# A short convolution and a maxout FFN on one core: the order of set-up work and first loads is changed

## The chip, the cores and the metric

The kernel runs on one core of a Trainium2 chip. The metric is the device time of one execution in microseconds. The engines of the core are named as the profile names them: PE (TensorE, matmuls; PEld is its weight load), DVE (VectorE), ACT (ScalarE), POOL (GpSimd) and SP (SyncE, which here does nothing but issue DMAs). Each engine works through its own instructions in order and waits on semaphores for the others.

## The reference

The input is x with 8 batches of 4160 rows of 192 channels. Eight heads of 24 channels each have 7 weights; a softmax over the 7 gives a causal filter that runs along the rows. The result goes through a maxout FFN with three input matrices.

```
w = exp(weight - max(weight)); w = w / (sum(w) + 1e-09)       # (8 heads, 7 taps)
y[b, s, h*24:(h+1)*24] = sum over k of w[h, k] * x_pad[b, s + k, h*24:(h+1)*24]
y = y.reshape(33280, 192)
h = maximum(maximum(y @ w1, y @ w2), y @ w3)                   # 192 -> 768
out = h @ w_out                                                # 768 -> 192
```

## The kernel before

The 33280 rows are cut into 65 blocks of 512 rows. For each block the kernel loads x, casts it to f16, runs the convolution as matmuls with a banded matrix of the softmax weights, and then two layers of matmuls. The maxout is rewritten: with wd = w1 - w3 and w2 - w3, h = y w3 + max(relu(y(w1 - w3)), y(w2 - w3)), and the part y w3 w_out is folded into a small matrix m = w3 w_out that is made once on the chip. So layer 1 (`l1`) needs two products per slice of 128 hidden channels, `top` takes relu on ACT and max on DVE, and layer 2 (`st2`) adds the hidden part and the m part in PSUM.

The first four blocks (`NDENSE = 4`) go another way, because they come before the pipeline is filled. Their x lies in five overlapping chunks of up to 112 rows (`chunks_of`). `cast_dense` (L211) writes the f16 copy into two tiles `xz[t][0]` and `xz[t][1]`, which must be zero where no channel of a head lies; blocks 2 and 3 use the tiles of blocks 0 and 1 again. `conv_dense` (L378) runs 80 matmuls of the chunks against `band`, and ACT and DVE evacuate the result into `yd` (L383). `l1_dense` (L526) then makes the layer-1 products of blocks 0 and 1.

From block 4 on, x lies in 16 pieces of 32 rows with overlap, in two halves of the partitions, in float32 buffers `xf`. There are seven such buffers (`XBUF = 7`). In the buffers of blocks 4 and up, partitions 32 to 63 must be zeroed before the load, since only some of them are written by it. `zero_x` does that, either as a copy of zeros on ACT (L137) or as a memset on a given engine (L134). The load of a block from 4 on is two DMAs of 234 KB (one for each half of the partitions). `cast_x` (L194, POOL) casts a buffer to f16.

The order of work on every engine is written out by hand (`manual_schedule`): what is issued first in the program runs first on its engine. All loads and stores go through the one queue of SP, in the order of the program, except the 7 softmax weights of each head (`wk`), which ACT issues. A load that has to wait for a zeroed buffer therefore holds up all DMAs that come after it in the program.

The set-up, in the order of the program:

- The loads: `wk` on ACT; then on SP x0 (420 KB in two DMAs), `load_wa` (L223: rows 0 to 127 of w3, w1 and w2, here columns 0 to 255), `load_wb` (L227: the other 64 rows), x1 (420 KB), the remaining columns of the weights, w_out (`wos`), x2 and x3.
- POOL makes an identity matrix. DVE zeroes `idle` (L247), `line` (L259), the two tiles `xz[0]` (L261) and `band` (L263).
- `keep_warm` issues matmuls on zeros so that PE is not idle: five of them before the softmax and three after the band matmuls.
- The softmax: maximum on DVE (L268), exp on ACT (L269, which makes the activation table be loaded first), sum (L271), reciprocal (L272) and the scaled filter `line` (L274) on DVE.
- 38 small matmuls (L283) spread `line` into the band pattern; ACT copies 28 of their columns and DVE 10 into the four row groups of `band` (L287).
- Between these, ACT zeroes buffers 4 and 5, and DVE zeroes the two tiles `xz[1]` (L276) and casts x0 (L211).

After the set-up come the dense products. `make_wd` (L302) subtracts w3 from w1 and w2 on DVE or POOL, `copy_w3` (L306), `cast_w3` (L310) and `cross_wd` (L313) move weights to where a product needs them, `transpose_w3` and `make_m` make m, and `first_hidden` is layer 2 of block 0. In the kernel before, buffer 6 is zeroed around the first `conv_dense`, and the loads of buffers 4, 5 and 6 are issued right after it. Then come the main loop over the blocks from 2 on, in which `conv` (L357), `l1` (L503) and `st2` (L567) are interleaved; `turn` (L411) transposes the convolution's result by DMA and `double` (L420, POOL) copies it to the other half of the partitions. The convolution of blocks 5 and 6, the first that needs their buffers, runs in the step of block 3.

Of the kernel before, what the change touches and what calls it, by code (L numbers as in the profile page):

```python
# [10 lines left out]
FP32 = mybir.dt.float32  # L11
FP16 = mybir.dt.float16
AXX = mybir.AxisListType.X
AF = mybir.ActivationFunctionType

P = 128
KW = 7
PAD = KW - 1
NHEAD = 8
GRP = 24  # L20
BAND_W = 128 + PAD
# [7 lines left out]
def kernel(  # L29
# [12 lines left out]
    nc = tc.nc  # L42
# [43 lines left out]
    NDENSE = 4  # L86
# [3 lines left out]
    NR = NBLK // TOK // 2  # L90
# [3 lines left out]
    def rows_of(t):  # L94
        rows = [(b, S + o) for (b, S, N, off) in blocks[t] for o in range(0, N, TOK)]
        assert len(rows) == 2 * NR
        return rows

    const = ctx.enter_context(tc.tile_pool(name="const", bufs=1))
# [10 lines left out]
    psp = ctx.enter_context(tc.tile_pool(name="psp", bufs=2, space=bass.MemoryType.PSUM))  # L110
# [5 lines left out]
    xin, xbuf, XBUF, loaded = {}, [], 7, set()  # L116

    def get_x(t):

        if not 0 <= t < NB or t in xin:  # L120
            return
        if t < XBUF:
            xbuf.append(const.tile([P, NR, D], FP32, name=f"xf_{t}"))
        xf = xbuf[t % XBUF if t < NDENSE + XBUF else NDENSE + (t - NDENSE - XBUF) % 3]
        assert all(v[0] is not xf for v in xin.values())
        xin[t] = [xf, 0, ()]

    def zero_x(t, q0=0, q1=NR, eng=None):

        if t >= NDENSE:  # L130
            get_x(t)
        xf = xbuf[t]
        if eng is not None:
            eng.memset(xf[TOK:HALF, q0:q1, :], 0.0)  # L134
            return
        zero = idle[TOK:HALF, 0:D]
        nc.scalar.copy(out=xf[TOK:HALF, q0:q1, :],  # L137
                       in_=bass.AP(tensor=zero.tensor, offset=zero.offset,
                                   ap=[list(zero.ap[0]), [0, q1 - q0], [1, D]]))

    def load_x(t, eng=nc.sync):
        if not 0 <= t < NB:
            return
        loaded.add(t)
        get_x(t)
        xf = xin[t][0]
        if t < NDENSE:
            todo = [(0, c[3], c[1] * SEQ + c[2], i) for i, c in enumerate(chunks_of[t])]
        else:
            todo = [(HALF * (i // NR) + (0 if s else LAP), KR if s else TOK,  # L150
                     b * SEQ + s - (LAP if s else 0), i % NR) for i, (b, s) in enumerate(rows_of(t))]
        parts = []
        i, n = 0, len(todo)
        row = [c[2] for c in todo]
        while i < n:
            k = i
            while k + 1 < n and todo[k + 1][:2] == todo[i][:2] and row[k + 1] - row[k] == row[i + 1] - row[i]:
                k += 1
            step = row[i + 1] - row[i] if k > i else 0
            p0, rlen, _, q0 = todo[i]  # L160
            q1 = todo[k][3] + 1
            src = bass.AP(tensor=x.tensor, offset=row[i] * D,
                          ap=[[D, rlen], [step * D, q1 - q0], [1, D]])
            eng.dma_start(out=xf[p0:p0 + rlen, q0:q1, :], in_=src)
            if parts and parts[-1][0] == rlen:
                parts[-1] = (rlen, parts[-1][1], q1)
            else:
                parts.append((rlen, q0, q1))
            i = k + 1
        xin[t] = [xf, todo[0][0], parts]  # L170
# [6 lines left out]
    def place(t):  # L177
        return pairs.get(t, (t, 0, 0))
# [3 lines left out]
    def cast_x(t):  # L182
        if not 0 <= t < NB:
            return
        xf, p0, _ = xin.pop(t)
        t0, u, nu = place(t)
        if u == 0:
            pool = x16q if nu == 4 else x16p
            x16s[t0] = pool.tile([P, NHEAD, 4, nu, 2, GRP], FP16, tag="x16", name=f"x16_{t0}")
        if p0:  # L190
            nc.gpsimd.memset(xf[0:p0, 0, :], 0.0)
        K = HALF + KR
        for r in range(2):
            nc.gpsimd.tensor_copy(out=x16s[t0][0:K, :, :, u, r, :].rearrange("p h j c -> p j h c"),  # L194
                                  in_=xf[0:K, 4 * r:4 * r + 4, :].rearrange("p j (h c) -> p j h c", c=GRP))
# [3 lines left out]
    xz = {t: [const.tile([P, NQ, D], FP16, name=f"xz_{t}_{v}") for v in range(2)] for t in range(2)}  # L199
    xz[2], xz[3] = xz[0], xz[1]  # L200

    def cast_dense(t, copies, slots_=range(CYC // 32)):
        xf, _, parts = xin.pop(t)
        for v, copy in enumerate(copies):
            if copy is None:
                continue
            for s in slots_:
                cut = GRP * (32 * s // GRP + 1)
                a, b = (32 * s, cut) if v == 0 else (cut, 32 * s + 32)
                for (rl, q0, q1) in parts:  # L210
                    copy(  # L211
                        out=xz[t][v][0:rl, q0:q1, :].rearrange("p q (k c) -> p q k c", c=CYC)[:, :, :, a:b],
                        in_=xf[0:rl, q0:q1, :].rearrange("p q (k c) -> p q k c", c=CYC)[:, :, :, a:b])
# [7 lines left out]
    def load_wa(f):  # L221
        for st, n, wsrc in ((w3s, 0, moe_w3), (ws, 0, moe_w1), (ws, 1, moe_w2)):
            nc.sync.dma_start(out=st[:, n, f], in_=wsrc[0:P, f])  # L223

    def load_wb(f):
        for st, lo, n, wsrc in ((w3s, 0, 1, moe_w3), (ws, 0, 2, moe_w1), (ws, HALF, 2, moe_w2)):
            nc.sync.dma_start(out=st[lo:lo + HALF, n, f], in_=wsrc[P:D, f])  # L227

    wk = const.tile([NHEAD, KW], FP32)
    nc.scalar.dma_start(out=wk[:], in_=weight)  # L230
    wos = const.tile([P, NJ, D], FP32)
    load_x(0)
    load_wa(slice(0, PW))
    load_wb(slice(0, PW))
    load_x(1)
    load_wa(slice(PW, 2 * PW))
    load_wb(slice(PW, DFF))
    load_wa(slice(2 * PW, DFF))
# [4 lines left out]
    make_identity(nc, ident[:])  # L243
    ident16 = const.tile([P, P], FP16)
    nc.gpsimd.tensor_copy(out=ident16[:], in_=ident[:])
    idle = const.tile([P, NBLK], FP16)
    nc.vector.memset(idle[:], 0.0)  # L247
    def keep_warm(n, pool=psw, tag="w"):

        ps = pool.tile([P, NBLK], FP32, tag=tag, name="idle")  # L250
        for _ in range(n):
            nc.tensor.matmul(ps[:], lhsT=idle[:, 0:P], rhs=idle[:], start=True, stop=True)
# [6 lines left out]
    nc.vector.memset(line[:], 0.0)  # L259
    for v in range(2):  # L260
        nc.vector.memset(xz[0][v][:], 0.0)  # L261
    band = const.tile([P, NHEAD, BAND_W], FP16)
    nc.vector.memset(band[:], 0.0)  # L263
    keep_warm(5, psp, "p")
    wexp = const.tile([NHEAD, KW + 1], FP32)
    nc.vector.memset(wexp[:], 1e-9)
    wneg = const.tile([NHEAD, 1], FP32)
    nc.vector.reduce_max(out=wneg[:], in_=wk[:], axis=AXX, negate=True)  # L268
    nc.scalar.activation(out=wexp[:, 0:KW], in_=wk[:], func=AF.Exp, bias=wneg[:])  # L269
    wrec = const.tile([NHEAD, 1], FP32)  # L270
    nc.vector.reduce_sum(out=wrec[:], in_=wexp[:], axis=AXX)  # L271
    nc.vector.reciprocal(out=wrec[:], in_=wrec[:])  # L272
    zero_x(4)
    nc.vector.tensor_scalar_mul(out=line[:, 31:31 + KW], in0=wexp[:, 0:KW], scalar1=wrec[:])  # L274
    for v in range(2):
        nc.vector.memset(xz[1][v][:], 0.0)  # L276
    cast_dense(0, (nc.vector.tensor_copy, nc.vector.tensor_copy))
    CUT = 28
    for lo, hi, copy in ((0, CUT, nc.scalar.copy), (CUT, WIN, nc.vector.tensor_copy)):
# [6 lines left out]
        for a in range(4):  # L286
            copy(out=band[32 * a:32 * a + 32, :, 32 * a + lo:32 * a + hi],  # L287
                 in_=bps[:, 0:hi - lo, :].rearrange("p c h -> p h c"))
    zero_x(5)
    keep_warm(3, psp, "p")  # L290


# [31 lines left out]
    def transpose_w3(pools):  # L324
        ps = [pool.tile([P, 2, 2 * P], FP32, tag=tag, name=f"pt{g}") for g, (pool, tag) in enumerate(pools)]
        for n in range(2):
            for j in range(NJ):
                nc.tensor.matmul(ps[j // 2][:, j % 2, P * n:P * (n + 1)], lhsT=w3h[:, n, P * j:P * (j + 1)],
                                 rhs=ident16[:], start=True, stop=True)
        for g in range(NJ // 2):  # L330
            nc.scalar.copy(out=w3t[:, 2 * g:2 * g + 2, :], in_=ps[g][:])
# [53 lines left out]
    def cross(t, copy=nc.vector.tensor_copy):  # L385

        yd = dense[t]
        for i in range(2):
            copy(out=yd[HALF * i:HALF * (i + 1), 1, :], in_=yd[HALF * (1 - i):HALF * (2 - i), 0, :])
# [140 lines left out]
    def tops(*tiles):  # L530
        for t, j in tiles:
            top(t, j, (open_ps[t, j, 0], open_ps[t, j, 1]))
# [143 lines left out]
    GP = nc.gpsimd.tensor_copy  # L676
    make_wd(0, 0, 2)
    make_wd(1, 0, 2)
    zero_x(6, 4, NR, nc.vector)
    conv_dense(0, (ACT, DVE))  # L680
    zero_x(6, 0, 4)
    for t in range(NDENSE, XBUF):
        load_x(t)
    copy_w3(DVE, 0, 2)
    make_wd(2, 0, 2)
    cast_dense(1, (GP, ACT), (1, 2, 0))
# [22 lines left out]
    cast_dense(2, (GP, GP))  # L709
    l1_dense([(1, 4, WW), (1, 5, WW)], "HF")  # L710
    tops((1, 4), (1, 5))
    transpose_w3((PQ[0], PQ[0], PQ[1]))
    cast_dense(3, (GP, GP))
    cross_wd(1, ACT)
# [1 line left out]
    first_hidden(1)  # L716
    conv_dense(2, (ACT, ACT), (WW[0], PQ[1]))
    cast_x(4)
    cross(2)
    make_m(0)  # L720
    make_m(1)
# [112 lines left out]
```

## Time and profile before

| | us |
|---|---|
| median of 3 runs | 454.37 (454.01 to 454.64) |
| the profiled execution | 454.51 |
| its span in the trace | 452.7 |
| PE busy | 446.8 (99% of the span) |
| DVE busy | 356.5 (79%) |
| ACT busy | 320.0 (71%) |
| POOL busy | 202.9 (45%) |
| bytes moved by DMA | 72.03 MB, mean 159 GB/s |

A line of a timeline or of the chain starts with the time from the span's start and the length, both in us; then come the engine, the line of the kernel, the instruction, what it writes and reads, and how often. What stands in brackets is the time that the engine sat idle before it and what ended that. L numbers are lines of the kernel before. A busy PE is not always a PE at full speed: matmuls are pipelined and their ends are modelled, so the distance between the starts of equal matmuls tells the speed.

### The profile page before, as it was taken

What the parts mean: (1) busy time and instruction counts of PE and PEld (TensorE: products, weight loads), DVE (VectorE), ACT (ScalarE), POOL (GpSimd) and SP (SyncE); (2) the same over time, 40 slices, a digit from 0 to 9 for tenths busy, and PEclk for the clock granted to TensorE, in tenths of its full rate; (3) what the DMA queues carried; (4) which work ended last, traced back from release to release, by engine and by line L of the source; (5) the groups of instructions that cost most, each with busy time, mean ns of one, the idle gap of its engine ahead of it and who ended that gap; (6) DMA issues with size and microseconds to landing.
All of it is one profiled execution on the core that took longest, in us unless ns stands there. A gap on an engine that the chain in (4) does not pass through costs nothing.

```text
span 452.7 us, 18493 instructions
## 1 busy us (share of the span) xinstructions
PE 446.8 (99%) x7702; PEld 412.6 (91%) x7702; DVE 356.5 (79%) x617; ACT 320.0 (71%) x604; POOL 202.9 (45%) x226
## 2 busy tenths in 40 slices
PE   7999999999999999999999999999999999999997
PEld 3569999999999999999999999999999999999996
DVE  7768778878878787887878788887878788787775
ACT  7767767767777676777767777776767777776664
POOL 2864836556454534645263464535346452505000
PEclk9999999999999999999999999999999999999999
DMA  7969997596875869587685949657594776535223
GB/s 205 231 178 166 199 205 195 146 206 180 169 180 147 168 129 207 138 176 185 118 190 141 210 117 184 177 136 186 133 206 124 178 189 118 117 89 104 59 72 106
DMA packets 127987, 72.03 MB, mean 159 GB/s; under 512 B 52064, under 2 KB 127711, under 8 KB 127903
## 3 DMA queue, kind: packets, MB, share of 16 engines
q1 hardware_dynamic: 127743, 70.75, 68.3%
q8 instruction: 60, 0.98, 1.0%
q14 instruction: 24, 0.20, 0.1%
q10 hardware_dynamic: 160, 0.10, 0.1%
HBM read 33.28 MB, written 25.56 MB: 130 GB/s over the span
## 4 chain that ended last, share of the span: by engine, by line
PE 97%; ACT 1%; DMA 0%; DVE 0%; issue 0%; ACTq 0%
PE po L567 36%; PE lq L503 31%; PE lp L503 22%; PE G L357 3%; PE lw L526 1%; PE lp L526 1%; PE D L378 1%; PE po L625 0%; PE po L598 0%; DMA wk<-in_weight_dram 0%; PE lq L526 0%; ACT xf L137 0%; ACT band L287 0%; ACT L269 0%; PE pm L337 0%; PE band L283 0%
## 5 line engine op out<-in xcount | busy, mean ns | idle before, releaser
L491 DVE TENSOR_TENSOR h<-r,lq 128x512 f16<-128x512 f16 x384 | 263.0, 686 | 85.1 <-ACT r L490 77.3
L567 PE MATMUL po<-wo,h 64*128 64x192 f16 x3024 | 329.8, 243 | 0.0
L490 ACT ACTIVATE r<-lp 128x512 f16<-128x512 f32 x384 | 229.0, 597 | 114.3 <-PE lp L503 100.8
L503 PE MATMUL lp<-yp,wd 64*128 64x512 f16 x1098 | 295.6, 376 | 0.0
L503 PE MATMUL lq<-yp,wd 64*128 64x512 f16 x1098 | 295.5, 376 | 0.0
L567 PEld LDWEIGHTS <-h 64*128 64x128 f16 x3024 | 240.9, 94 | 6.3 <-issue 4.1
L503 PEld LDWEIGHTS <-wd 64*128 64x128 f16 x2268 | 177.7, 94 | 10.6 <-issue 0.2
L194 POOL CAST x<-xf 103x768 f16<-103x768 f32 x122 | 97.5, 827 | 106.6 <-DMA xf<-in_x_dram 93.0
L567 PE MATMUL po<-m,yp 64*128 64x192 f16 x720 | 141.0, 243 | 0.0
L420 POOL COPY yp<-yp 64x1536 f16<-64x1536 f16 (+1 forms) x62 | 89.6, 1445 | 96.2 <-DMA yp<-ys 75.9
L575 DVE TENSOR_TENSOR o<-a,po 128x384 f32<-128x384 f32 x126 | 69.0, 547 | 0.0
L567 PEld LDWEIGHTS <-yp 64*128 64x128 f16 x720 | 66.3, 94 | 0.5
L574 ACT COPY a<-po 128x384 f32<-128x384 f32 x126 | 59.5, 472 | 0.0
L397 ACT CAST ys<-G 128x384 f16<-128x384 f32 x61 | 26.3, 482 | 9.5 <-PE G L357 9.4
L397 DVE CAST ys<-G 128x384 f16<-128x384 f32 x61 | 31.0, 550 | 0.0
L357 PE MATMUL G<-x,band 39*32 39x192 f16 (+2 forms) x1152 | 17.3, 234 | 0.0
L357 PEld LDWEIGHTS <-band 39*32 39x32 f16 x1152 | 10.7, 91 | 5.2 <-issue 4.7
L503 PE MATMUL lp<-yd,wd 64*128 64x512 f16 x36 | 9.7, 376 | 0.0
L503 PE MATMUL lq<-yd,wd 64*128 64x512 f16 x36 | 9.7, 376 | 0.0
L526 PEld LDWEIGHTS <-wd 128*128 128x128 f16 (+1 forms) x48 | 3.2, 98 | 5.7 <-issue 2.4
L211 POOL CAST xz<-xf 112x160 f16<-112x160 f32 (+2 forms) x15 | 4.1, 319 | 7.7 <-DMA xf<-in_x_dram 7.7
L378 PEld LDWEIGHTS <-xz 112*32 112x32 f16 x320 | 4.6, 107 | 2.7 <-issue 1.0
(74 smaller groups left out, 98.2 us busy)
## 6 DMA issues: line engine op xcount, KB each, us to landing
xf<-in_x_dram SPq DMA_DIRECT2D x113, 234.0 KB
out_dram<-o SPq DMA_DIRECT2D x62, 384.0 KB
xf<-in_x_dram SPq DMA_DIRECT2D x7, 204.8 KB
xf<-in_x_dram SPq DMA_DIRECT2D x3, 420.0 KB
ws<-in_moe_w_dram SPq DMA_DIRECT2D x8, 128.0 KB
yp<-ys SPq DMA_TRANSPOSE x62
out_dram<-o SPq DMA_DIRECT2D x5, 192.0 KB
wos<-in_moe_w_out_dram SPq DMA_DIRECT2D x1, 576.0 KB
```

Source lines behind the costliest of these rows:

```text
L194: nc.gpsimd.tensor_copy(out=x16s[t0][0:K, :, :, u, r, :].rearrange("p h j c -> p j h c"), in_=xf[0:K, 4 * r:4 * r + 4, :].rearrange("p j ( ...
L357: nc.tensor.matmul(G[2 * (k // per) + i][TOK * j:TOK * (j + 1), k % per, :], lhsT=band[row, h, HALF * i + LAP:HALF * i + KR], rhs=x16s[t0] ...
L378: nc.tensor.matmul(ps[32 * g:32 * g + 32, lo:hi], lhsT=xz[t][v][0:rlen, q, 32 * s:32 * s + 32], rhs=band[0:rlen, h, cc:cc + hi - lo], star ...
L397: copy(out=slots[t][:, i % 2, :, :, GRP * h0:GRP * (h0 + per)].rearrange("p u r (h c) -> p h (u r) c", c=GRP), in_=G[i][:].rearrange("p h ...
L420: nc.gpsimd.tensor_copy(out=yp[HALF * i:HALF * (i + 1), 1, :, :, :, :].rearrange("p i u k n -> p (i u k n)"), in_=yp[HALF * (1 - i):HALF * ...
L490: nc.scalar.activation(out=r[:], in_=ps[0][:], func=AF.Relu)
L491: nc.vector.tensor_max(out=hs[t][:, j, :], in0=r[:], in1=ps[1][:])
L503: nc.tensor.matmul(ps[i][:], lhsT=w_of(i, c, j), rhs=y_all(t, i, c), start=(n == 0), stop=(n == NC - 1))
L526: nc.tensor.matmul(open_ps[t, j, i][:], lhsT=a, rhs=b, start=(t, j, i) not in begun, stop=(t, j, i) in begun)
L567: nc.tensor.matmul(ps[b0, i][:, s % 2, :], lhsT=a, rhs=b, start=first, stop=last)
L574: nc.scalar.copy(out=a[:], in_=ps[s - 1, 0][:])
L575: nc.vector.tensor_add(out=outs[t][:, s - 1:s + 1, :], in0=a[:], in1=ps[s - 1, 1][:])
```

## The change

Six things are done. A new one-element tile `warm` is zeroed by DVE, and ACT takes its exp before anything else, so that the activation table is loaded for that. In SP's queue x1 is put ahead of the 64-row part of the first weights. The zeroing of the two tiles `xz[1]` goes from DVE to POOL, behind the identity. The softmax's maximum and exp are put ahead of the zeroing of `band`. The zeroing of buffer 5 (before: ACT, whole, behind the band copies) goes to DVE behind the last `tops` of blocks 0 and 1, and its load follows there. The zeroing of buffer 6 (before: half on DVE, half on ACT, around the first `conv_dense`) goes to POOL behind `cast_x(4)`, and its load follows there. The load of buffer 4 stays where it was.

```diff
     wk = const.tile([NHEAD, KW], FP32)
     nc.scalar.dma_start(out=wk[:], in_=weight)
+    warm = const.tile([1, 1], FP32)
+    nc.vector.memset(warm[:], 0.0)
+    nc.scalar.activation(out=warm[:], in_=warm[:], func=AF.Exp)
     wos = const.tile([P, NJ, D], FP32)
     load_x(0)
     load_wa(slice(0, PW))
+    load_x(1)
     load_wb(slice(0, PW))
-    load_x(1)
     load_wa(slice(PW, 2 * PW))
@@
     nc.gpsimd.tensor_copy(out=ident16[:], in_=ident[:])
+    for v in range(2):
+        nc.gpsimd.memset(xz[1][v][:], 0.0)
@@
     for v in range(2):
         nc.vector.memset(xz[0][v][:], 0.0)
-    band = const.tile([P, NHEAD, BAND_W], FP16)
-    nc.vector.memset(band[:], 0.0)
-    keep_warm(5, psp, "p")
     wexp = const.tile([NHEAD, KW + 1], FP32)
     nc.vector.memset(wexp[:], 1e-9)
     wneg = const.tile([NHEAD, 1], FP32)
     nc.vector.reduce_max(out=wneg[:], in_=wk[:], axis=AXX, negate=True)
     nc.scalar.activation(out=wexp[:, 0:KW], in_=wk[:], func=AF.Exp, bias=wneg[:])
+    band = const.tile([P, NHEAD, BAND_W], FP16)
+    nc.vector.memset(band[:], 0.0)
+    keep_warm(5, psp, "p")
     wrec = const.tile([NHEAD, 1], FP32)
@@
     nc.vector.tensor_scalar_mul(out=line[:, 31:31 + KW], in0=wexp[:, 0:KW], scalar1=wrec[:])
-    for v in range(2):
-        nc.vector.memset(xz[1][v][:], 0.0)
     cast_dense(0, (nc.vector.tensor_copy, nc.vector.tensor_copy))
@@
-    zero_x(5)
     keep_warm(3, psp, "p")
@@
-    zero_x(6, 4, NR, nc.vector)
     conv_dense(0, (ACT, DVE))
-    zero_x(6, 0, 4)
-    for t in range(NDENSE, XBUF):
-        load_x(t)
+    load_x(4)
     copy_w3(DVE, 0, 2)
@@
     tops((1, 4), (1, 5))
+    zero_x(5, 0, NR, nc.vector)
+    load_x(5)
     transpose_w3((PQ[0], PQ[0], PQ[1]))
@@
     cast_x(4)
+    zero_x(6, 0, NR, nc.gpsimd)
+    load_x(6)
     cross(2)
```

## The prediction

> **What bounds the kernel now.** I read the page's engine shares and chain first, then the chain of its first 48 us, then the order of events on the other engines up to 24 us.
>
> ```profile
> PE 446.8 (99%) x7702; PEld 412.6 (91%) x7702; DVE 356.5 (79%) x617; ACT 320.0 (71%) x604; POOL 202.9 (45%) x226
> ...
> PE 97%; ACT 1%; DMA 0%; DVE 0%; issue 0%; ACTq 0%
> ```
>
> TensorE is busy for 99% of the span and 97% of the chain that ended last. An edit that touches no matmul can only move the moment from which TensorE runs without a break. The chain of the first 48 us shows that moment:
>
> ```profile
> 0.75 1.69 DMA wk<-in_weight_dram
> 2.50 1.28 ACT L269
> 3.80 0.31 ACT wexp L269
> ...
> 4.50 0.23 DVE line L274
> 4.78 0.94 PE band L283 x28
> ...
> 7.14 1.48 ACT xf L137
> 8.64 0.59 ACT yd L383
> 9.27 0.58 PE lp L526
> ```
>
> The head waits for the 7 softmax weights (landed 2.44), then for the exp table (1.28 us), then for exp, sum, reciprocal and line. Band matmuls start at 4.78. Later the zeroing of buffer 5 (7.14, ACT) holds up the first dense evacuation. From 9.27 on the chain is TensorE. The timeline, with start, length and what ended the wait before:
>
> ```profile
> 1.20 2.32 PE L252 MATMUL idle<-idle 128*128 128x512 f16 x5 [1.20 <-DVE idle L247]
> ...
> 4.76 0.97 DVE L276 MEMSET xz<- 128x480 uint32 x2
> ...
> 5.66 0.92 DVE L211 CAST xz<-xf 112x240 f16<-112x240 f32 x6
> ...
> 6.50 0.97 DVE L287 CAST band<-band 32x80 f16<-32x80 f32 x4
> ...
> 7.29 1.91 PE L378 MATMUL D<-band,xz 112*32 112x103 f16 x80
> ...
> 9.39 0.86 POOL L211 CAST xz<-xf 112x160 f16<-112x160 f32 x3 [7.72 <-DMA xf<-in_x_dram]
> ...
> 10.96 1.11 PE L378 MATMUL D<-band,xz 112*32 112x103 f16 x80
> ...
> 13.40 2.79 POOL L302 TENSOR_TENSOR wd<-ws,w3s 128x256 f16<-128x256 f32 x4 [1.40 <-DMA ws<-in_moe_w_dram]
> ```
>
> Two things are to be seen. The first dense convolution (7.29) starts where three chains meet: the idle matmuls, ACT's band copies (end 7.11), and DVE's row of zeroing, casts and band copies. And the same 80 matmuls take 1.91 us at 7.29 but 1.11 us at 10.96: TensorE runs at half speed until about 10.9, while the clock row reads full throughout. That is 6.1 us after the band matmuls began.
>
> **The change, part by part.**
>
> Exp table early: the dummy exp waits only for a one-element DVE memset (0.07 to 0.12 by the 8-row memsets; it pushes the idle matmuls from 1.20 to 1.28). ACT issues the wk load until 0.75 + 0.58 = 1.33, loads the table until 2.61, does the dummy by 2.91 (the exp row, 0.30). DVE, with the band memset moved behind, has the maximum at 2.65 (wk at 2.44). The real exp then runs from 2.91 instead of 3.80, 0.89 earlier; with start gaps 0.90, taken. From exp to line 0.70 us of DVE work remain; the moved band memset (0.51, 2.65 to 3.16) fits before the sum at 3.23. Bands start at 3.88.
>
> [...] This trace shows 1283 ns for the load and exp 0.02 us behind its end; the measurement decides.
>
> TensorE from bands to dense took 4.78 to 7.29 = 2.51, so 6.39 now. ACT's buffer-4 zeroing (1.47) runs 3.22 to 4.69, before its band copies (4.84 to 6.21). DVE loses the second zeroing (0.97): line ends at 3.83, then casts and band copies, 1.82 us (5.66 to 7.48). It keeps up if x0 has landed by 4.55. The trace bounds that landing: after 3.45 (420 KB are x0; the DMA had moved that much) and before 5.66 (DVE did not wait). x1 landed about 0.85 us after its bytes had moved (8.5 against 9.36); the same lag gives 4.3. Taken: no loss; worst end, all 0.90 lost.
>
> xz[1] zeroing on POOL: between 0.4 us each (slope of its two f32 memsets, 0.206 for 128 and 0.248 for 192 elements) and 1.0 (its cast of 1152 elements, 1.145). POOL sat idle 7.72 us before 9.39, so zero. Without that cover, up to 2 us on x1's cast.
>
> x1 before the 64-row weights: x1 takes their place in SP's queue (3.17 instead of 5.06), landing near 7.5, and its casts (POOL 0.86, ACT 0.96) leave the path of the dense matmuls at 10.96. The 64-row weights are issued 0.62 later and finish no later than x1 did, 9.36, because the byte position is the same. DVE needs them for its copy at 10.01 (9.1 now): 0 to 0.7 late, with 0.9 of slack to the matmuls at 12.00 (11.1 now). Zero.
>
> Buffer zeroings off ACT (1.48 at 7.14, 0.83 at 9.25) and DVE (0.70 at 8.48): the first lets the l1 matmul start at the end of the dense ones, as it does at 12.00, not at 9.27: 0.10 gained. The others only fill time beside TensorE.
>
> Late zeroings: DVE takes 32x1536 in about 1.34 (0.538 for 576, 0.698 for 768), inside its 2.37 us gap after 21.6. Uncovered, 1.34 late for the crossing copies at 23.98. POOL about 1.1 after cast 4 (ends 24.21), up to 1.65 at its cast's rate.
>
> Late loads, two DMAs of 234 KB for each buffer: SP, which ran through buffer 6 by 19.6, now stands until DVE has zeroed buffer 5 (about 22) and POOL buffer 6 (25.3). Queued behind the two waits: x7, the first store, x8, the transposes of 32.43. x7 waits for ACT's zeroing of buffer 0 until 25.9 already and is issued about 26 either way, so nothing behind it moves. x5 lands near 25.7 (its issue 1.2, then 2 to 3 us, bounded by x1's 4.3 from issue to landing with a full queue ahead of it), x6 near 29. Cast 5 (was 24.72) may hold back POOL's crossing at 28.73; cast 6 is needed by the convolution at 36.93. Slack about 5 us: zero.
>
> Sum: 0.90 + 0.10 = 1.00. The profiled execution took 454.51 (span 452.7 and 1.8 around it), so 453.5; the median of the runs is 0.14 lower: 453.4.
>
> **The clock step.** If it follows the start of the bands (3.88 + 6.1 = 10.0), everything shifts by 1.0. If it stays at 10.9, the 0.90 is worked at half speed: gain 0.45 to 0.55. If the idle gap, 1.26 us now (3.52 to 4.78) and 0.28 then (3.60 to 3.88), is short enough not to count, the step comes 1.28 + 6.1 = 7.4. Then 1.0 us runs slow instead of 3.6: gain 0.90 + 1.3 = 2.2, cut by the weights that POOL subtracts at 13.40 (ready 14.1, used at 15.05: 0.95 of slack, plus up to 1.0 if the DMA's slack stretch at 5.5 to 7.0, 78 GB/s in its last us, fills up).
>
> [...]
>
> **Rivals.**
> - Early step, 7.4: gain 1.0 to 2.0, 452.4 to 453.4, about 452.8. For it: the gap nearly closes. Against: the bands use 8 rows and may not count.
> - Fixed step, or x0 late: gain 0 to 0.5, about 454.0. For it: DVE's chain was one of three that met at 7.29.
> - Slower: x6 becomes a wait. If its landing, with POOL's cast behind it (1.6) and that of buffer 5 before, passes about 34, the convolution of 36.93 (35.9 now) waits us for us; from 35 on it eats the gain, at 36 it gives 455.4. Against: its estimate is 29.
> - The change does nothing because the table waits for wk anyway, as at 2.50: 454.3, inside the second.
>
> **How the numbers follow.** Whole shift (453.4) 0.44, early step 0.27, fixed step or late x0 0.14, slower 0.15. 0.2% (0.91 us) is about what a measurement of this kernel can tell, so the line is 453.46. The whole shift, 1.0 with some tenths either way, falls past it in 0.29 and short of it in 0.15. Faster 0.29 + 0.27 = 0.56; same 0.15 + 0.14 = 0.29; slower 0.15. Range: 452.4, the early step's end, to 454.9, which takes in the loss of all gain and the slower case's start. The likeliest case's own range is 453.1 to 453.7.
>
> **What would show it.** Table load starting near 1.33, bands at 3.88, first dense matmuls at 6.4, x1's cast before 9, no DVE wait before the x0 casts or one under 0.5. The matmul pitch tells the step: 0.43 or 0.215 us at l1's first products. Wrong if TensorE waits for POOL's wd near 14, or at the convolution of 36.

## The result and the profile after

The changed kernel takes 458.34 us (median of 4 runs, 457.51 to 459.70) where the kernel before takes 454.34 (4 runs, 454.01 to 454.64). The ratio is 1.0093, with an interval of 1.0079 to 1.0106: slower by 4.0 us, where 453.4 had been forecast. The profiled execution took 459.70, with a span of 457.9 against 452.7, so it has 5.2 us to explain, somewhat more than the median has.

From the page of the kernel after, first the engines (busy time, share of the span, instructions), then the granted clock by slices, a queue, and the chain by engine:

```profile
PE 449.9 (98%) x7702; PEld 412.4 (90%) x7702; DVE 357.9 (78%) x616; ACT 318.1 (69%) x603; POOL 205.5 (45%) x229
...
PEclk9999989999999999999999999999999999999999
...
q8 instruction: 60, 0.98, 1.0%
...
PE 94%; DMA 2%; POOL 1%; issue 1%; SPq 1%; DVE 0%; POOLq 0%
```

TensorE has the same 7702 matmuls and fills less of the chain: 94% instead of 97%. "issue" has gone from 0% to 1%. The clock row dips once, in the slice near 60 us. The queue named "instruction" will matter below.

The set-up did what was forecast of it. The timeline of the kernel after, engine by engine (ACT, DVE, PE, POOL; start, length, what ended the wait before):

```profile
1.37 1.28 ACT L233 ACT_TABLE_LOAD   x1 [1.37 <-PEq L821]
2.66 0.20 ACT L233 ACTIVATE warm<-warm 1x1 f32<-1x1 f32 x1
...
3.46 0.22 DVE L279 TENSOR_SCALAR line<-wexp,wrec 8x7 f16<-8x7 f32 x1
4.29 1.00 DVE L211 CAST xz<-xf 112x240 f16<-112x240 f32 x6 [0.61 <-DMA xf<-in_x_dram]
...
9.46 0.28 DVE L308 COPY w3s<-w3s 64x256 f32<-64x256 f32 x1 [0.52 <-DMA w3s<-in_moe_w_dram]
...
3.73 1.20 PE L286 MATMUL band<-ident,line 8*32 8x32 f16 x38 [0.19 <-DVE line L279]
...
6.25 1.91 PE L380 MATMUL D<-band,xz 112*32 112x103 f16 x80
...
13.49 1.41 POOL L304 TENSOR_TENSOR wd<-ws,w3s 128x256 f16<-128x256 f32 x2 [0.27 <-DMA ws<-in_moe_w_dram]
15.60 1.41 POOL L304 TENSOR_TENSOR wd<-ws,w3s 128x256 f16<-128x256 f32 x2 [0.71 <-DMA ws<-in_moe_w_dram]
...
27.21 1.59 POOL L194 CAST x<-xf 103x768 f16<-103x768 f32 x2 [0.44 <-DMA xf<-in_x_dram]
...
32.00 1.59 POOL L194 CAST x<-xf 103x768 f16<-103x768 f32 x2 [1.86 <-DMA xf<-in_x_dram]
```

Bands start at 3.73 instead of 4.78 and the first dense convolution at 6.25 instead of 7.29, a lead of 1.04 us. The two `wd` lines on POOL show where part of it went: before, the four subtractions ran in one piece from 13.40; now they wait for weights twice. Those weights are late because SP's queue stood still behind x1. The DMAs that SP issues in the kernel after:

```profile
7.10 0.47 SPq L227 DMA_DIRECT2D w3s<-in_moe_w_dram  x1
9.15 1.76 SPq L227 DMA_DIRECT2D ws<-in_moe_w_dram  x2
```

The second should follow at 7.6 (before, the pair went at 7.19 and 7.71) and comes at 9.15. The weight path then goes through POOL to layer 2 of block 0 (L598, now L600). TensorE's timeline there, before and after:

```profile
20.59 2.14 PE L598 MATMUL po<-wo,h 128*128 128x192 f16 x24
```

```profile
20.14 2.14 PE L600 MATMUL po<-wo,h 128*128 128x192 f16 x24
```

Of 1.04 us, 0.45 are left. The transposes just ahead of it (L328, now L330) had still started 0.74 earlier (19.18 instead of 19.92), so 0.29 went into the wait for POOL. Another 0.24 had gone in the second dense convolution, which took 1.35 us instead of 1.11, since part of it ran at a slower pace: there four matmuls took 0.08 us up to 10.5 and 0.045 behind that.

The rest of the loss lies behind that, in the chain that ended last (start, length, engine, line; the longest pieces of the whole span):

```profile
43.75 0.45 PE G L359 x41
44.20 1.15 issue
45.35 0.32 PE G L359 x23
...
58.82 0.44 PE G L359 x40
59.27 1.80 issue
61.07 0.32 PE G L359 x24
...
76.33 0.39 issue
```

TensorE stops in the middle of a convolution, after 41 or 40 of its 64 matmuls, and the profile finds nothing that it waits for. Before, these convolutions ran through:

```profile
44.14 0.68 PE G L357 x64
...
57.65 0.68 PE G L357 x64
```

The list of waits of the kernel after (in all, times, longest) says the same in two lines; before they read 4.7 us with a longest of 0.2, and no such line for the matmuls:

```profile
PEld L359 <- issue: 8.4, 33, 1.9
...
PE G L359 <- issue: 3.3, 3, 1.8
```

But the kind of stall was there before. This is the chain of the kernel before:

```profile
27.38 0.90 PE D L378 x59
28.28 0.40 issue
28.68 0.34 PE D L378 x13
```

The windows of 10 us (PE, PEld, DVE, ACT, POOL busy, granted clock, DMA share, GB/s), the kernel after and then the kernel before:

```profile
30.00:40.00 10.00, 9.83 (x251) 7.89 (x251) 7.56 (x14) 6.55 (x14) 3.44 (x6) 1.00 1.16 194
...
60.00:70.00 10.00, 8.93 (x128) 8.18 (x129) 5.29 (x10) 4.80 (x9) 3.20 (x4) 0.83 1.05 168
```

```profile
30.00:40.00 10.00, 9.98 (x257) 8.26 (x255) 7.56 (x14) 7.10 (x14) 5.63 (x9) 1.00 0.64 162
...
60.00:70.00 10.00, 10.00 (x155) 9.71 (x152) 8.02 (x14) 7.10 (x14) 4.58 (x6) 1.00 0.89 212
```

Two things are to be seen. The DMA share from 30 to 40 us has risen from 0.64 to 1.16, while the bytes rose only from 162 to 194 GB/s. SP issued the load of buffer 5 at 22.61 (14.84 before) and that of buffer 6 at 26.80 (17.13 before), and the load of block 7 behind it went at 27.67 instead of 25.94, so the same traffic comes later. Why it also takes more of the engines' time for a byte is not shown. And right after the stall of 1.80 us the granted clock falls to 0.83 over 10 us: it is 0.50 from 62 to 65, and the same stretch of TensorE's program takes 9.03 us instead of 7.48.

Followed at the same instruction in both traces, the kernel after leads by 1.08 us near 32 (its lead grew again from 0.45, since the kernel before lost 0.6 between 23 and 29 us, where it has its stall of 0.40). From there it loses 0.41 to about 37.5, 1.63 to 45.4 (1.15 of it the stall), 0.15 to 53, 2.07 to 61 (1.80 the stall), 1.55 to 70 (the half clock) and 0.48 by the last convolution (0.39 the stall): together 6.29, so it ends 5.21 behind. Four stalls make 3.49 of that (the fourth is 0.15 at 37.33, seen in the chain of that stretch), the half clock 1.55, short gaps the remaining 1.25.

### The profile page after: what moved, and what is told of

The parts are those of the page before. It is cut to its first block, busy times and chain, and to the rows that moved or that the text cites. A ratio compares the mean times of both kernels' runs of the same rounds, so it can differ in the third digit from the quotient of the medians.

```text
span 457.9 us, 18492 instructions
## 1 busy us (share of the span) xinstructions
PE 449.9 (98%) x7702; PEld 412.4 (90%) x7702; DVE 357.9 (78%) x616; ACT 318.1 (69%) x603; POOL 205.5 (45%) x229
## 4 chain that ended last, share of the span: by engine, by line
PE 94%; DMA 2%; POOL 1%; issue 1%; SPq 1%; DVE 0%; POOLq 0%
PE po L569 36%; PE lq L505 31%; PE lp L505 22%; PE G L359 3%; DMA xf<-in_x_dram 1%; DMA ws<-in_moe_w_dram 1%; POOL wd L304 1%; PE po L600 0%; PE D L380 0%; PE po L627 0%; SPq L223 0%; POOL wo L697 0%; PE pm L339 0%; POOL w3h L312 0%; SPq L164 0%
```

## Where the stalls sit

Count TensorE's weight loads and matmuls in program order, 15,404 in all. The stalls of TensorE without a releaser behind 20 us, in this trace and in those below, sit at number 191 plus a multiple of 256 (959, 1215, 1471, 1727, 2239, 2751): the first three exactly, the others one, two and three numbers short of it, by the same amount in every trace. What shifts these is open. (One of 0.16 at 215 us in e2 is 14 short.) The shorter ones ahead of 20 us, where TensorE also waits for weights and casts, are not all at such numbers and are left out here. The queue "q8 instruction" carried 60 packets and 0.98 MB, that is 16.3 KB for each and one packet for 257 of TensorE's instructions. Up to 15,404 there are 60 numbers of the form 191 plus a multiple of 256, as many as packets. From these counts the packets are taken here for TensorE's program, which is the author's estimate: no record names the engine that a packet is for, nor the DMA engine that carried it. The page counts the packets of q1, which carries x, and of q8 as shares of the same 16 engines.

The times of the packets fit this. In the table, "reached" is when TensorE passes a boundary in the trace, "packet" is the start of the next packet on q8 (to 0.1 us), and "next reached" is when TensorE passes the boundary after it. In the stalled cases of all traces it goes on 2.4 to 3.5 us behind the packet, but for two (3.7 in e7 and 4.5 in e8, both at 1471). And in none of the 18 traces of this case, stalled or not, does TensorE pass a boundary between 959 and 3263 less than 2.3 us behind its packet.

| kernel | boundary | reached | packet | next reached | stall there |
|---|---|---|---|---|---|
| before | 703 | 23.37 | 25.80 | 28.68 | 0.40 |
| before | 1215 | 33.24 | 34.30 | 38.15 | none |
| before | 1983 | 51.86 | 53.27 | 57.90 | none |
| after | 1215 | 32.16 | 34.73 | 37.48 | 0.15 |
| after | 1471 | 37.48 | 42.88 | 45.37 | 1.15 |
| after | 1983 | 52.97 | 58.17 | 61.08 | 1.80 |

Unhindered, TensorE needs 4.5 to 7.5 us from one boundary to the next in this part of the program. If the packet comes 1 to 1.5 us after the boundary was reached, that covers it; if it comes 5 us after, it doesn't. Two windows of the transfer queues of the kernel after (packets, MB, share of 16 engines), 37.5 to 42.8 and 42.8 to 43.0, show the longest delay:

```profile
q1 hardware_dynamic: 1505, 0.91, 128.8%
```

```profile
q1 hardware_dynamic: 94, 0.05, 84.9%
q8 instruction: 1, 0.02, 29.6%
```

For 5.3 us data packets fill the engines and no instruction packet is among them. That is a coincidence in time so far, not yet a cause. Full engines alone don't delay the packet either: from 51.8 to 53.3 the data packets of the kernel before have a share of 103.8%, and its packet starts 1.5 us after boundary 1983 was reached. In the kernel after they have 98.3% from 52.97 to 58.17, and the packet takes 5.2 us.

## The experiments

All ratios are to the kernel before, run on the same chip in the same round.

**The two halves of the change.** The first has only the late zeroings and loads, the second only the set-up.

```diff
 # e1_late_only, against before
-    zero_x(5)                       # in the set-up
-    zero_x(6, 4, NR, nc.vector)
     conv_dense(0, (ACT, DVE))
-    zero_x(6, 0, 4)
-    for t in range(NDENSE, XBUF):
-        load_x(t)
+    load_x(4)
...
     tops((1, 4), (1, 5))
+    zero_x(5, 0, NR, nc.vector)
+    load_x(5)
...
     cast_x(4)
+    zero_x(6, 0, NR, nc.gpsimd)
+    load_x(6)
 # e2_setup_only: the change without these lines
```

> The kernel before with only the late zeroing and loading of buffers 5 and 6. Theory A (the late loads crowd the DMA engines from 28 us on, and TensorE's own instructions then arrive late): the stalls without a releaser come back near 38, 45 and 60 us, 457 to 459. Theory B (the faster set-up is what goes wrong: TensorE, 1 us ahead, runs into data and instructions that are not there yet; the late loads are harmless): 454.2 to 454.6, no such stall.

> The changed kernel with the zeroing and the loads of buffers 5 and 6 back where they were; exp table early, x1 ahead and xz[1] on POOL stay. Theory A: no stalls, 453.3 to 454.0 (the head's 1.05 less what late weights cost near 14 to 20 us). Theory B: 456 to 459, the stalls stay.

The late loads alone: 457.67 us, 1.0069 (1.0050 to 1.0087). The set-up alone: 456.49, 1.0055 (1.0035 to 1.0075). So each half loses by itself, and together they cost less than their sum. The chain of the first, then that of the second:

```profile
35.82 0.68 PE G L356 x64
37.24 2.09 issue
```

```profile
27.41 2.59 issue
```

With the late loads the stall is at boundary 1471 (packet 35.98, 3.9 us after 1215 was reached), and the granted clock falls behind it as after the 1.80: its means are 0.60 from 40 to 42 us and 0.54 from 42 to 44. With the loads in their old place the set-up stalls at 959 instead: 703 was reached at 22.52, the packet came at 27.41. The DMA share from 20 to 30 us is 0.92 there and 0.75 in the kernel before.

**Zeroing on GpSimd, loads early.** Would it help to keep the loads early and zero buffers 5 and 6 on the idle POOL?

```diff
 # e3_pool_zero, against after: buffers 4 to 6 loaded behind conv_dense(0), late zeroings out
     zero_x(4)
+    zero_x(5, 0, NR, nc.gpsimd)
+    zero_x(6, 0, NR, nc.gpsimd)
```

> The changed kernel with buffers 5 and 6 zeroed by POOL right behind xz[1] (POOL is idle from 3.3 to 9.3 us) and loaded early as before, so ACT and DVE stay free of it. Theory A: no stalls, 453.2 to 454.0. Theory B: 456 to 459.

459.03 us, 1.0104 (1.0067 to 1.0142), with a stall of 2.86 at 959. It brought something else to light, in the DVE's timeline:

```profile
3.44 1.35 DVE L281 TENSOR_SCALAR line<-wexp,wrec 8x7 f16<-8x7 f32 x1
4.48 2.41 DVE L211 CAST xz<-xf 112x240 f16<-112x240 f32 x6
```

In the kernel after these take 0.22 and 1.00 us. POOL's two memsets of 32x1536 f32 ran from 3.40 to 6.23, over both. The lead of the set-up was gone by the first dense convolution (7.58, against 7.29 in the kernel before). Not every operation of DVE was slowed beside such memsets: in e9 (below) they ran from 1.73 to 4.26, and DVE's sum and reciprocal at 3.79 and 3.98 took 0.15 each, as in the kernel before.

**Does the stall follow the instruction number?** The kernel after gets 32 more instructions ahead of everything: 17 small matmuls take the place of one idle one.

```diff
 # e4_shift16, against after
-    keep_warm(5, psp, "p")
+    keep_warm(4, psp, "p")
+    small = psp.tile([P, NBLK], FP32, tag="p", name="idle")
+    for _ in range(17):
+        nc.tensor.matmul(small[:, 0:32], lhsT=idle[:, 0:P], rhs=idle[:, 0:32], start=True, stop=True)
```

> The changed kernel with one idle matmul of 512 columns replaced by 17 of 32 columns, so that every later TensorE instruction moves on by 32 (16 loads and 16 matmuls) at about the same time. If the stalls inside the convolution are waits for the next piece of 256 instructions, they come 16 matmuls earlier in it: after 24 or 25 of 64 instead of 40 or 41. If the convolution waits for data or for a buffer, they stay after 40 or 41.

457.48 us in a single run. The chain:

```profile
36.54 0.58 PE G L362 x57
37.13 1.16 issue
38.28 0.23 PE G L362 x7
...
44.98 0.27 PE G L362 x25
45.34 0.54 PE G L362 x39
...
73.39 0.25 PE G L362 x24
73.64 0.64 issue
```

The breaks moved by 16 pairs of load and matmul, from after the 41st and 40th matmul to after the 25th and 24th. Boundary 1471 now falls into a convolution and stalls it after its 57th. (Of these breaks the one at 45.25 is only 0.09 long.) Here the place of a stall was set by the instruction's number, not by the tile, the load or the semaphore that stood there.

**The set-up's parts, and traffic by itself.** The set-up was split into x1's place and the early exp; a third kernel adds only the late load of buffer 6 to the early exp; a fourth leaves the kernel before as it is and adds 468 KB that nothing waits for, behind the load of block 7.

```diff
 # e5_x1_ahead, against before
     load_wa(slice(0, PW))
+    load_x(1)
     load_wb(slice(0, PW))
-    load_x(1)
 # e6_exp_early: warm exp, xz[1] on POOL, band's zeroing behind the exp; loads as before
 # e8_x6_late: e6 with buffer 6 zeroed and loaded behind cast_x(4), as in the change
 # e7_extra_traffic, against before
     load_x(7)
+    extra()     # two DMAs of 234 KB from x into columns of ws that are not read any more
```

> The kernel before with only x1 put ahead of the 64-row weights. Theory C (TensorE's next 256 instructions come by a DMA that waits behind the loads; what counts is how full the DMA engines are when TensorE asks): SP stands still between 7.6 and about 9 us, all later loads come about 1 us later, the piece asked for near 23.4 us arrives near 27 instead of 25.8, TensorE stands still before 30: 455.0 to 456.5. Rival (the order of x1 is harmless, and only the exp's head start brings the stall): 454.0 to 454.5.

> The kernel before with the exp table early, the softmax ahead of band's zeroing, and xz[1] zeroed by POOL; the order of the loads as before. Theory C with x1's order as the only culprit of the set-up: the piece comes near 25.5 and TensorE goes on near 28.4 as before, so that only a few tenths of the head's 0.9 us are left: 453.6 to 454.3. Rival (a head start of TensorE costs in itself): 455 to 457.

> The kernel before with one more load of 468 KB, of x into weights that are no longer read, behind the load of block 7 (about 27 us), which is about where buffer 6 is loaded in the changed kernel. Nothing waits for it. Theory C: the pieces asked for near 33 and 38 us come 1 to 3 us later, TensorE stands still at instruction 1471: 455 to 458. Rival (it is the late arrival of x5 and x6, or the waits on SP, and not the traffic): 454.0 to 454.5.

> The kernel of the run e6_exp_early with buffer 6 alone zeroed on POOL behind cast 4 and loaded there. Theory C: the piece asked for near 23 us now comes earlier (no load of x6 ahead of it), that of 32 to 38 us later: 454 to 458 with a stall at instruction 1471 or 1727. Rival (late x5 does the harm): 453.3 to 454, no stall.

| kernel | median us | ratio | interval | stalls in the profiled execution |
|---|---|---|---|---|
| e5, x1 ahead | 455.33 | 1.0018 | 1.0003 to 1.0032 | 1.18 at 959 |
| e6, exp early | 455.75 | 1.0039 | 1.0011 to 1.0068 | 1.57 at 959 |
| e8, and x6 late | 458.31 | 1.0078 | 1.0060 to 1.0097 | 1.71 at 1215, 0.47 at 1471, 0.88 at 1727, 0.21 at 2239 |
| e7, extra traffic | 457.46 | 1.0058 | 1.0039 to 1.0077 | 0.34 at 1471 |

The extra traffic is the plainest result: no computing engine gets an instruction more and nothing waits for the data, and 3 us are lost. Its profiled execution was its fastest (455.19), so it shows little of the loss; and its stall of 0.34 fits badly, as TensorE went on 3.75 us behind the packet. The early exp was a miss: 453.6 to 454.3 was expected. Its lead of 1 us at the bands was mostly gone by 10.60, where the second dense convolution began, held up by x1 (10.96 before), and the stall at 959 came on top. Why the DMA engines moved 155 and 165 GB/s there from 20 to 22 and 22 to 24 us (share 0.98 and 0.92), where in the kernel before they moved 210 and 222 (0.91 both), was not settled. e5's time was in its range, but its packet for 959 came at 26.1 and not near 27; TensorE reached 703 at 22.75, 0.6 earlier than in the first trace of the kernel before, and so stood longer. e8 was expected between 454 and 458 and has its stalls where x6 was moved, with x5 loaded early; a late x5 is not needed for them.

**Choosing the time of x6's load.** If loads beside certain boundaries are what costs, a load in a quiet place should cost nothing. In the first of these, buffers 5 and 6 are zeroed on POOL early and x6 is loaded near 23 us; in the second all loads are early; the third adds the early exp to the first. The fourth is the change without the stores of blocks 0 to 2.

```diff
 # e9_x6_at_23, against before (zeroings of 5 and 6 at their old places out)
+    zero_x(5, 0, NR, nc.gpsimd)        # behind zero_x(4)
+    zero_x(6, 0, NR - 1, nc.gpsimd)
...
+    load_x(4)                          # behind conv_dense(0)
+    load_x(5)
...
     cross_wd(1, ACT)
+    zero_x(6, NR - 1, NR)
+    load_x(6)
 # e10_zero_pool: buffer 6 zeroed on POOL altogether, loads 4 to 6 behind conv_dense(0)
 # e11_exp_x6_at_23: e9 with e6
 # e12_no_stores, against after, in store()
-        if t < 0:
+        if t < 3:
             return
```

> The kernel before with buffer 5 and seven eighths of buffer 6 zeroed by POOL behind the identity, so that ACT and DVE are free of it; buffers 4 and 5 are loaded early as before, buffer 6 when ACT has zeroed its last eighth near 23.2 us, which is just behind TensorE's request for the piece that starts at instruction 959 (near 22.8). Theory C: that piece comes by 24.5, no stall at 959, and the load of x6 is over before the next request at 27.6, so that it meets no later one: 453.2 to 454.0. If any later load of x6 harms: 455 to 458.

> The same zeroing on POOL, but all of buffers 4 to 6 loaded early as before. Theory C: TensorE reaches instruction 703 about 0.6 us sooner than before, its next piece still comes near 25.8 because the loads stand in front of it, and it waits longer at 959: no gain, 454.0 to 455.0. Rival (the zeroing on ACT and DVE was worth its time): 453.4 to 453.9.

> The run e9_x6_at_23 with the exp table early, the softmax ahead of band's zeroing and xz[1] zeroed by POOL. Theory C: the head's 1.0 us is eaten by the wait for x1 (landing 9.4 to 10.1) as in e6_exp_early, and the rest as in e9_x6_at_23: 453.0 to 454.2. If a faster head costs in itself: 455 to 457.

> The changed kernel without the stores of blocks 0, 1 and 2 (384 KB each, near 28.6, 36.4 and 44.4 us; their rows of the output are left out). Theory C: the pieces asked for near 32, 37 and 45 us come 1 to 3 us sooner and the stalls at 1471 and 1727 shrink: 454 to 457. Rival (not the traffic on the DMA engines but waits on SP's queue or on data): 458, stalls unchanged.

| kernel | median us | ratio | interval |
|---|---|---|---|
| e9, x6 near 23 us | 453.95 | 0.9994 | 0.9982 to 1.0005 |
| e10, loads early | 454.17 | 0.9991 | 0.9982 to 1.0000 |
| e11, e9 and exp early | 456.06 | 1.0035 | 1.0015 to 1.0056 |
| e12, without three stores | 460.11 | 1.0120 | 1.0101 to 1.0139 |

The first two have no stall at a boundary from 20 us on in their traces, but a second trace of the kernel before (e13 below) has none either, and their gain is within what a measurement can tell. e10's time was in its range, though the longer wait at 959 that was expected did not come. The convolutions of the first run through, in its chain:

```profile
30.81 0.60 PE G L358 x64
36.53 0.68 PE G L358 x63
43.67 0.68 PE G L358 x64
```

They start 0.44 to 0.47 earlier than before, which is the old stall of 0.40 at 959. e11 lost its head as e3 did: POOL's memsets lay over DVE's small operations (the scaled filter took 1.35 us, and the first dense convolution began at 7.42). In its profiled execution it then had a stall of 1.67 at 2751, which is most of what it is slower there.

e12 was the clearest miss: fewer bytes, and no faster than the kernel after (1.0120 against 1.0093; the intervals just overlap). Its chain has the longest stall of all, at 1471:

```profile
38.03 3.24 issue
```

With no store between them the loads x6, x7 and x8 follow each other in SP's queue. From 30 to 32 us the DMA share is 0.91 at 145 GB/s, where the kernel before has 0.59 at 191. So bytes alone don't tell the delay. That loads in a row take longer for a byte is not shown either: the kernel after, with a store between them, has 1.11 at 192 in the same stretch. What else makes the packet so late here is open.

**Moving the stall by moving the traffic.** The same 468 KB were put ahead of the load of block 7, near 20 us; and in e1 the load of block 8 was moved behind the first transposes. The kernel before was profiled again beside them, and the early exp was run with x6 held until near 23 us.

```diff
 # e14_extra_early, against before
+    extra()
     load_x(7)
 # e16_x8_behind, against e1
-                load_x(8)
                 cast_x(6)
...
                 turn(4)
+                load_x(8)
                 load_x(9)
 # e15_exp_hold, against e6: the last eighth of buffer 6 that ACT zeroes, and the load of x6, go behind cross_wd(1, ACT)
```

> The kernel before once more, for a second trace. 453.3 to 455.6. If the arrival of instruction pieces is a property of the order of the loads, the pieces come within 0.5 us of the first trace (25.8, 30.5, 34.3, 40.7); if it is noise of the DMA pace, they differ by 1 us or more.

> The kernel before with the extra load of 468 KB of e7_extra_traffic, but ahead of the load of block 7 and so right behind that of block 6 (about 20 us, no transpose before 32). Theory C: the piece asked for at 23.4 comes 1 to 2.5 us later, TensorE stands still at instruction 959 and no longer at 1471: 455 to 457. Rival (only traffic together with the transposes of 32 us and later does harm): 454.0 to 455.0.

> The kernel of e6_exp_early (exp table early, softmax first, xz[1] on POOL) with the load of buffer 6 held back until ACT has zeroed its last eighth near 23.2 us; nothing large is zeroed on POOL. Theory C: the request at 23.2 no longer stands behind x6, the stall at 959 goes, and what is left of the head's gain shows: 453.2 to 454.3. Rival (the earlier exp costs in itself): 455.3 to 457.

> The kernel of e1_late_only with the load of x8 moved behind the first transposes (from about 29 to 35 us). Theory C (the request at 32 waits behind the loads of x6, x7 and x8): its piece comes 1 to 2 us sooner and the stall of 2.1 us at instruction 1471 shrinks to under 1: 455 to 457, unless the cast of x8 becomes late. Rival (it waits for the transposes): unchanged, 457 to 458.

e14: 457.07 us, 1.0058 (1.0038 to 1.0078). Its stall is at 959 and not at 1471 (a second one, of 0.51, is at 2239); it is in the chain:

```profile
27.87 2.88 issue
```

703 was reached at 22.98, the packet came at 27.84, TensorE went on at 30.77. The same extra bytes at two places of the queue cost the same 0.58%, and in the traces each has its stall at the boundary that lies beside it.

e16: 455.98, 1.0031 (1.0005 to 1.0057), against 1.0069 for e1. The stall of 2.09 at 1471 is gone, and one of 0.74 at 1215 has come. Taking one load from beside the boundary gave back half of the loss.

e13, the kernel before: 453.48 in one run, and no stall at 959; its packet came at 24.34 instead of 25.80. So the packets of one and the same kernel differ by 1.4 us here between executions, and by 2.4 for boundary 1727 (45.5 instead of 47.9). The kernel before sits at the edge: the stall is 0.4 us of the 1.0 that its two profiled executions differ by. In the same round three of its 24 runs took 457.05 to 458.02 us, each with a mean granted clock of 0.996, like the profiled execution of the kernel after; where they lost the time is not on record.

e15: 455.60, 1.0018 (0.9988 to 1.0048), no stall at 959, but one of 1.15 at 70.35 (boundary 2751). It doesn't decide anything; in no run did the early exp bring a gain that reached the end.

## Why the prediction was wrong

**Right.** The table load at 1.37 (1.33 forecast), the bands at 3.73 (3.88), x0's landing at 4.29 (4.3), the first dense convolution at 6.25 (6.39). The next operation on ACT started at 2.66, 0.01 us behind the table load's end, so the row of 1283 ns stands. DVE's zeroing took 1.34 (1.34), POOL's 1.37 (1.1 to 1.65), the two `xz[1]` on POOL 0.86 each (0.4 to 1.0), hidden as said. DVE waited 0.61 for x0, a little over the 0.5 that was named as a sign; the dense convolution did not start later for it.

**Too small.** x1 landed near 9.2, not 7.5. "The 64-row weights ... finish no later than x1 did ... Zero" was costed by DVE's wait alone; DVE did wait (0.52 and 0.45), but what counted is that SP stood from 7.57 to 9.15, so that all later weights came later. That took 0.29 us of the lead by layer 2 of block 0, as TensorE's wait for POOL's copy of w_out (`wo`, ready at 20.09). In e5, where x1's place is the only edit, SP stands from 7.59 to 9.24 too, and it loses 0.18%. So ahead of all the stalls the lead was 0.45 us, and not the 1.00 of the sum.

**The clock step.** The slower pace of TensorE lasted in the kernel before up to 10.5 at least (its matmuls of 128x512 start 0.43 us apart up to 10.51, and the 80 of the next convolution, from 10.96, took 1.11 us). In the kernel after it ended at 10.5, within the second dense convolution (1.35 us for its 80 matmuls, between 1.91 and 1.11). In e6 it was over at 8.22, where the matmuls of 128x512 start 0.22 apart. So its end lay more than 2 us apart in three traces; in the second dense convolution it cost 0.24 us of the lead, which the sum has at nothing, and it could not be forecast from one trace. What ends it is not shown, and the granted clock reads 1.00 throughout that stretch. That the granted clock would fall to 0.50 in the middle of the run, at 62 us, wasn't foreseen.

**The step that failed.** "Late loads, two DMAs of 234 KB for each buffer ... so nothing behind it moves ... Slack about 5 us: zero." Its landings were set 1.5 and 3 us too early (x5 at 27.2 where 25.7 was forecast, x6 at 32.0 where 29 was), and still the convolution never waited for either. The slack was real and beside the point. One link of it was wrong in SP's queue too: x7 was to be issued about 26 either way, and was issued at 27.67 instead of 25.94, behind x6 at 26.80. The step asked only who needs x5 and x6, and not what else comes by DMA in the time to which they were moved. By the counts of the packets, TensorE's own program does. With 936 KB, which had been issued before 20 us, issued from 22.6 and 26.8 us on, the DMA share from 30 to 40 us rose from 0.64 to 1.16, and the packet of 1471 came over 5 us after its boundary was reached. So did that of 1983, but the moved loads had landed 20 us before, and the share from 50 to 60 us is 1.02 against 0.98; how the change leads to the stall of 1.80 there, and to the granted clock of 0.50 behind it, is not shown. e1 puts a price of 0.69% on this step alone; e7 and e14 show that traffic is enough for it, e4 that the stalls sit at the boundaries, e16 that a load taken away gives about half of it back. Beneath this step lies the premise of the first part, that an edit which touches no matmul "can only move the moment from which TensorE runs without a break": here such an edit added breaks of 3.49 us in the profiled execution.

The row that should have given warning was in the profile before: a stall of 0.40 us called "issue" at 28.28, in the middle of a stream of matmuls and with no releaser. The prediction passed over it, as 0% of the chain.

**The rivals.** The slower rival had the right sign and the wrong mechanism: x6 as a wait of the convolution near 36, which never came. "The change does nothing because the table waits" was wrong: the table no longer waits for `wk`. The early step and the fixed step both spoke of the first 11 us, and what decided lay behind 27.

**What stays open.** What the 2.4 to 3.5 us between packet and going on are made of; what, besides the bytes, makes a packet late (e12, and boundary 1983 in the kernel after); why e6's loads ran slower; and how many of the other executions' losses are stalls and how many half clock. Of the four runs of the kernel after, two have a mean granted clock of 0.996 (459.70 and 458.31 us) and two of 1.000 (457.51 and 458.36), so the half clock is not needed for the loss.

## What to carry to other kernels

A transfer that nobody waits for was not free here: 468 KB that no engine needed cost 0.58% in e7 and in e14. When TensorE runs through its instructions without a break, its program, for which the q8 packets are taken, has to come in time too: with two loads moved into a busy stretch, the packet came 5.4 us after 1471 was reached, where the kernel before has 2.6 (40.7 and 38.15). Look in the chain and the waits for "issue" in the middle of dense matmuls, count loads and matmuls to it, and if the stalls lie 256 apart as here, look at the q8 packets and try to move a transfer away from just behind a boundary (e16 gained by it; e12, which left three stores out, did not). A lead won in the head (1 us at the bands in e6, which ended 0.39% slower) counts only once it has been followed to a place behind the last such boundary with heavy traffic.

## What the runs showed of the hardware

- The queue "q8 instruction" carried 60 packets of 16.3 KB, one for 257 of TensorE's loads and matmuls; its stalls without a releaser behind 20 us lay at 191 plus multiples of 256, up to three numbers short (14 in one case). Over the 18 traces the packet started between 1.0 us before and 5.4 us after TensorE reached the boundary before, and after a stall TensorE mostly went on 2.4 to 3.5 us behind it. Between 959 and 3263 it never passed a boundary less than 2.3 us behind the packet.
- After the stall of 1.80 us in the kernel after the granted clock was 0.50 for 3.4 us, from 61.7 to 65.1, and TensorE was busy for all of 62 to 65. After those of 2.09 in e1 and 3.24 in e12 it had means of 0.60 and 0.54 (40 to 44 us) and of 0.58 and 0.56 (42 to 46). Other stalls, of 1.15 (after), 2.59 (e2), 2.86 (e3) and 2.88 us (e14), were followed by windows at 1.00.
- Beside POOL memsets of 32x1536 f32 some DVE operations took longer: the scaled filter 1.35 us in e3 and in e11, not 0.22, and six casts 2.41 in e3, not 1.00. Others kept their times beside them: the sum and the reciprocal their 0.15 each and the memset of `band` its 0.51 (in e9).
- With x1 (420 KB) issued at 3.15 us, SP's queue issued nothing from 7.57 to 9.15 in the kernel after. In the kernel before, with x1 issued at 5.06, it issued the same two loads at 7.19 and 7.71.
